# A Fourier mixing layer and a SoLU feed-forward on one core: every second unit's down product as seven block products

## The chip, the cores and the metric

The kernel runs on one core of a Trainium2 chip. The metric is the device time of one execution in microseconds (us); the time before is the median of three runs. Five engines work side by side, each in the order of its own instructions, and wait for each other by semaphores: TensorE (PE in the profile; its weight loads are listed apart as PEld), VectorE (DVE), ScalarE (ACT), GpSimd (POOL) and SyncE (SP), which here only issues transfers.

## The reference

```python
# x: (8, 3136, 256) float32
X = np.fft.fft(np.fft.fft(x, axis=1), axis=2).real     # mixing
x = X.reshape(25088, 256)
h = x @ w_in                                           # 256 -> 1024, "up"
e = np.exp(h - max(h)); sm = e / (sum(e) + 1e-9)       # over the 1024 of a row
solu = h * sm
ln = (solu - mean(solu)) / sqrt(var(solu) + 1e-6) * g_ln
out = ln @ w_out                                       # 1024 -> 256, "down"
```

Everything is float32.

## The kernel before

The sequence of 3136 is 49 x 64. A first transform (over 49) is written to DRAM and read back turned (`turn`); a second one (over 64) gives tiles `q` of 128 tokens. The transform over the 256 features is folded into `w_in`. Two of the eight sequences make a pair; there are four pairs of 25 *units*. A unit stands for one frequency `k1` and its mirror: both share the even and the odd part of `h`, so a unit has two *signs* (the unit with `k1 = 0` has one), and each sign is 128 tokens x 1024.

```python
units = [Unit(p, k1) for p in range(NP) for k1 in range(NK)]     # 4 x 25 = 100
lag = 4

def up(t, c):                       # c = 0: even part, c = 1: odd part; 512 columns a matmul
    for half in range(2):
        nc.tensor.matmul(ps[:, fs], t.q[:, c * P : (c + 1) * P], Wi[:, c, fs], ...)

def spread(t):                      # one value of q to all partitions, by SyncE's queue
    nc.sync.dma_start(out=t.r, in_=t.q[0:1, P : 2 * P])

def even(t, ps):                    # VectorE: ev = w_mid * r + (even part)
    nc.vector.scalar_tensor_tensor(out=t.ev, in0=w_mid, scalar=t.r, in1=ps, ...)

def join(t, ps):                    # VectorE: both signs of h, and the row maxima
def expo(t):                        # ScalarE: u = exp(h - max), both signs, with the sums
def product(t, s):                  # VectorE: u = h * u, with the sums
def square(t, s):                   # ScalarE: sums of squares
def stats(t):                       # GpSimd: five small instructions, then rs = v ** -0.5

def turn_blocks(t, s):              # VectorE: 32 x 32 transposes of u into v
    nc.vector.transpose(out=t.batch.v[:, t.w, :, o], in_=t.u[s])

def move_blocks(batch, units, engines=(nc.sync,)):     # 16 transfers finish the transposition
    for i in range(4):
        for q in range(4):
            engines[i % len(engines)].dma_start(out=uT[b, i], in_=v[a, q])

def down(t, s):                     # 8 matmuls of 256 columns
    ps = ps_m.tile([P, D], FP32, tag="m", name="ps_o")
    for c in range(KF):
        nc.tensor.matmul(ps, uT[:, c, :, s], Wo[:, c, :], start=(c == 0), stop=(c == KF - 1))

def scale(t, s, ps):                # ScalarE: ot = rs * ps
```

Two units share a batch, that is one buffer `v` and one buffer `uT`; of each there are two. PSUM holds the even and the odd part (two banks each) and four more banks, `ps_m`, which all other products take in turn. The steps run over the units; a step works on unit `i` and on the down products of unit `i - 4`:

```python
for i in range(len(units) + lag):
    store(units[i - lag - 1])                    # output rows of an older unit
    even(cur, up(cur, 0)); cur.odd = up(cur, 1)  # begin(i)
    take2(nxt, transform2(...)); spread(nxt)     # q and r of unit i + 2
    join(cur, cur.odd)
    expo(cur)
    ahead_pe(...)                                # a first transform of the next pair, in some steps
    ps_o = [down(old, s) for s in order]
    for s in cur.signs: product(cur, s)
    for s in cur.signs: square(cur, s); turn_blocks(cur, s)
    scale(old, order[0], ps_o[0])
    if cur.w: move_blocks(batches[-1], slice(0, 2))   # after the second unit of a batch
    stats(cur)
    ahead(...)                                   # loads and folds for the next pair
    scale(old, order[1], ps_o[1])
# (cut: the first four units, the last two, the setup of weights and tables)
```

Of the kernel before, what the change touches and what calls it, by code (L numbers as in the profile page):

```python
# [17 lines left out]
P = 128  # L18
# [17 lines left out]
def kernel(  # L36
# [34 lines left out]
    gpool = ctx.enter_context(tc.tile_pool(name="gpool", bufs=6))  # L71
# [5 lines left out]
    ps_m = ctx.enter_context(tc.tile_pool(name="ps_m", bufs=4, space=PSUM))  # L77
# [5 lines left out]
    Wo = const.tile([P, KF, D], FP32, name="Wo")  # L83
    ones = const.tile([P, P], FP32, name="ones")
# [7 lines left out]

    class Pair:
        def __init__(self, p):
            self.p = p
            self.raw, self.y, self.y0 = {}, {}, None
            self.g, self.zs = {}, {}
# [45 lines left out]
    def transform1(pr, s):  # L145

        c, l = divmod(2 * s, CH)
        if s == 0:  # L150
            pr.zd = dram.tile([ZR, NH, D], FP32, tag="zd", name="zd")
        if l == 0:

            if pr.p or c < 2:
                pr.z = zpool.tile([ZR, CH, D], FP32, tag="z", name="z")
            elif c < 4:
                z = fpool.tile([P, FF], FP32, tag="u", name="z_u", bufs=2)
                pr.z = z[0:ZR].rearrange("p (l d) -> p l d", l=CH)
            else:
                pr.z = gpool.tile([P, KG, D], FP32, tag="g", name="z_g")[0:ZR, 0:CH, :]  # L160
            pr.zs[c] = pr.z
        y = pr.y[c]
        ps = ps_m.tile([P, 2, D], FP32, tag="m", name="ps1")
        if s == NH // 2 - 1:
            parts = [(ps[0:ZR, 0], y[:, l], 0), (ps[0:ZR, 1], pr.y0[:, 0], 1), (ps[0:ZR, 1], y[:, l + 1], 2)]
        else:
            parts = [(ps[0:ZR], y[:, l : l + 2], 0)]
        first = True
        for o, i, t in parts:
            for h, cs in enumerate((EVEN, ODD)):  # L170
                nc.tensor.matmul(o[..., cs], F[:, 2 * t + h, :], i[..., cs], start=first, stop=True,  # L171
                                 skip_group_check=True)
                first = False
        nc.scalar.copy(pr.z[:, l : l + 2, :], ps[0:ZR])
        if l == CH - 2:
            keep(pr, c, slice(0, ZR if pr.p else 4 * KG))
# [12 lines left out]
    def transform2(pr, k1):  # L189

        i, k = divmod(k1, KG)
        g = pr.g[i]
        table = T[0][:, :, k, :] if i == 0 else T[1][:, :, k1 - KG, :]
        ps = ps_m.tile([P, KD * P], FP32, tag="m", name="ps2")
        for h in range(KD):
            o = ps[:, h * P : (h + 1) * P].rearrange("p (b k) -> p b k", b=2)
            nc.tensor.matmul(o, g[:, k, h * P : (h + 1) * P], table,  # L199
                             start=(h == 0), stop=True, skip_group_check=True)  # L200
        return ps
# [34 lines left out]
    def join(t, ps):  # L236

        t.nmax = small.tile([P, 2], FP32, tag="nmax", name="nmax")
        for s in t.signs:
            t.h[s] = fpool.tile([P, FF], FP32, tag="h", name="h", bufs=2)  # L240
            nc.vector.tensor_tensor_reduce(out=t.h[s], in0=t.h[0] if s else t.ev, in1=ps,  # L241
                                           scale=1.0 if s else -0.5, scalar=-3.0e38, op0=ALU.add, op1=ALU.max,
                                           accum_out=t.nmax[:, s : s + 1])

    def expo(t):
        t.esum = small.tile([P, 2], FP32, tag="esum", name="esum")
        t.neg = small.tile([P, 2], FP32, tag="neg", name="neg")
        for s in t.signs:
            nc.scalar.mul(out=t.neg[:, s : s + 1], in_=t.nmax[:, s : s + 1], mul=-1.0)  # L249
            t.u[s] = fpool.tile([P, FF], FP32, tag="u", name="u", bufs=2)  # L250
            nc.scalar.activation(out=t.u[s], in_=t.h[s], func=ACT.Exp, bias=t.neg[:, s : s + 1],  # L251
                                 accum_out=t.esum[:, s : s + 1])
# [15 lines left out]
    def stats(t):  # L268

        n = slice(0, len(t.signs))  # L270
        es = small.tile([P, 2], FP32, tag="es", name="es")
        nc.gpsimd.tensor_scalar(out=es[:, n], in0=t.esum[:, n], scalar1=1e-9, scalar2=1e-3,  # L272
                                op0=ALU.add, op1=ALU.mult)
        es2 = small.tile([P, 2], FP32, tag="es2", name="es2")
        nc.gpsimd.tensor_tensor(out=es2[:, n], in0=es[:, n], in1=es[:, n], op=ALU.mult)
        v = small.tile([P, 2], FP32, tag="v", name="v")
        nc.gpsimd.tensor_scalar(out=v[:, n], in0=t.ssq[:, n], scalar1=float(FF) ** -3, scalar2=None, op0=ALU.mult)  # L277
        nc.gpsimd.tensor_tensor(out=v[:, n], in0=v[:, n], in1=es2[:, n], op=ALU.add)
        t.rs = small.tile([P, 2], FP32, tag="rs", name="rs")
        nc.gpsimd.tensor_tensor(out=t.rs[:, n], in0=v[:, n], in1=neg_half[:, n], op=ALU.pow)  # L280
# [14 lines left out]
    def turn_whole(t):  # L295
# [4 lines left out]
        for s in t.signs:  # L300
            for half in range(2):
                ps = ps_m.tile([P, n, P], FP32, tag="m", name="ps_t")
# [17 lines left out]

    def down(t, s):
        uT = t.batch.uT[:, t.w].rearrange("p c i (n s) -> p c (i n) s", s=2)
        ps = ps_m.tile([P, D], FP32, tag="m", name="ps_o")
        for c in range(KF):
            nc.tensor.matmul(ps, uT[:, c, :, s], Wo[:, c, :], start=(c == 0), stop=(c == KF - 1))  # L325
        return ps

    def scale(t, s, ps):
        t.ot[s] = fpool.tile([P, D], FP32, tag="ot", name="ot", bufs=6)
        nc.scalar.mul(out=t.ot[s], in_=ps, mul=t.rs[:, s : s + 1])  # L330
# [21 lines left out]
    mantissa = const.tile([P, NW], I32, name="mantissa")  # L352
    limits = const.tile([P, 3], FP32, name="limits")
# [12 lines left out]
    def exponent(w, raw):  # L366

        if w.dtype == FP32:
            return None
        unit = qpool.tile([P, NW], I32, tag="unit", name="unit", bufs=3)  # L370
        bits(unit, raw[:, 1 : 2 * NW : 2], 20, ALU.logical_shift_right, 0x7FF, ALU.bitwise_and)
        return unit
# [36 lines left out]
    class Weights:  # L409
# [72 lines left out]
        def centre(self):  # L482

            cs = ps_m.tile([P, D], FP32, tag="m", name="cs")
# [25 lines left out]
    def ahead_pe(pr, step):  # L510
# [5 lines left out]
        if 0 <= step - 20 < NK // KG:  # L516
            turn(pr, step - 20)

    with tc.manual_schedule():
# [24 lines left out]
        for i, limit in enumerate((-896.0, 255.0, 255.0 * 2.0 ** 23)):  # L544
# [57 lines left out]
        def begin(i):  # L602

            cur = units[i]
            if i % 2 == 0:
                batches.append(Batch(i >= whole))
            cur.batch, cur.w = batches[-1], i % 2
            even(cur, up(cur, 0))
            cur.odd = up(cur, 1)
            if i + 2 < len(units):  # L610
                nxt = units[i + 2]
                take2(nxt, transform2(pairs[nxt.p], nxt.k1))
                spread(nxt)
# [3 lines left out]
        for i in range(len(units) + lag):  # L617
            cur = units[i] if i < len(units) else None
            old = units[i - lag] if i >= lag else None
            ahd = pairs[cur.p + 1] if cur and cur.p + 1 < NP else None  # L620
            last = i >= len(units) - 2
            prv = units[i - 1] if 0 < i <= whole else None
            if i > lag:
                store(units[i - lag - 1])
            if cur and i > whole:
                begin(i)
            if prv:
                turn_whole(prv)
            if cur:
                join(cur, cur.odd)  # L630
# [3 lines left out]
            if cur:  # L634
                expo(cur)
            if ahd:
                ahead_pe(ahd, cur.k1)
            if old:
                order = old.signs[::-1] if old is units[-1] else old.signs
                ps_o = [down(old, s) for s in order]  # L640
            if i == 0:

                weights.narrow_out(3)
            if cur:
                for s in cur.signs:
                    product(cur, s)
                    if i < whole and s == 0:
                        square(cur, s)
                if i == 1:
                    weights.centre()  # L650
                if i < whole:

                    begin(i + 1)
                for s in cur.signs:
                    if i >= whole or s:
                        square(cur, s)
                    if i >= whole:
                        turn_blocks(cur, s)
            if old:
                scale(old, order[0], ps_o[0])  # L660
            if cur:
                if last:
                    move_blocks(batches[-1], slice(cur.w, cur.w + 1), (nc.sync, nc.gpsimd) if cur.w else (nc.sync,))
                elif cur.w and i >= whole:
                    move_blocks(batches[-1], slice(0, 2))
                stats(cur)
            if i == 0:
                turn(first, 1, nc.sync)
            elif i in (5, 8, 11):
                turn(first, (i + 1) // 3)  # L670
            if ahd:
                ahead(ahd, cur.k1)
            if old and 1 in old.signs:
                scale(old, order[1], ps_o[1])
        store(units[-1])
# [76 lines left out]
```

## Time and profile before

| | before |
|---|---|
| median of three runs | 1188.7 us (1187.45 to 1188.8) |
| span in the profile | 1189.0 us |
| granted TensorE clock | 1.00 |
| uT moves | 752 transfers of 128 KB and 32 of 64 KB |
| SyncE's queue (q1) | 444608 packets, 146.22 MB |
| GpSimd's queue (q0) | 13760 packets, 38.16 MB |

How to read the lines below. In the first part of the page each engine has its busy time, the share of the span and the number of instructions. The chain that ended last is followed back from the last instruction to what released each step, and gives shares of the span by engine and by source line. A line of the timeline has the start, the time from the first start to the last end, the engine (SPq is SyncE's queue), the source line of the kernel, the operation, output <- inputs, the shape and the number merged. In brackets stands the idle time before it and who ended it. The ends of matmuls are modelled and overlap the next one's start, so the pace is read from start to start.

Source lines before: L227 `up`, L199 second transform, L171 first transform, L325 `down`, L233 `even`, L241 `join`, L258 `product`, L293 transposes, L319 `move_blocks`, L210 `spread`, L341 and L337 stores, L330 `scale`.

### The profile page before, as it was taken

Reading aid. Unit: us, or ns where it says so; the run is one execution under the profiler, and the core shown is the slowest. Engines: PE = TensorE matmul, PEld = TensorE weight load, DVE = VectorE, ACT = ScalarE, POOL = GpSimd, SP = SyncE. Lnnn points to the kernel's source line nnn. Section 1 sums busy time; section 2 is a strip of 40 time slices with the busy share of each in tenths; the row PEclk is TensorE's granted clock in tenths of the full one; section 3 lists DMA queues with packets and bytes.
Section 4 is the critical chain, followed back from the end, with each engine's and each line's share of the span. In section 5 each row is a group of like instructions: output and inputs, shape, how many; then the busy total and the mean of one; then the engine's idle time right before and its main releaser. Section 6 shows DMA issues by size and latency. Waiting matters only on the chain.

```text
span 1189.0 us, 15738 instructions
## 1 busy us (share of the span) xinstructions
PE 1152.6 (97%) x4720; PEld 874.5 (74%) x4720; DVE 912.3 (77%) x1234; ACT 679.9 (57%) x1404; POOL 505.9 (43%) x766
## 2 busy tenths in 40 slices
PE   2989999999999999999999999999999999999998
PEld 1556777778777777777777777777777777777787
DVE  6879777777768877787778978777786887877780
ACT  3566665656546656565556656565564665655561
POOL 3025556444544444442644554443553333333323
PEclk9999999999999999999999999999999999999999
DMA  9671989958996766655996887775897464554544
GB/s 231 199 188 27 191 187 193 196 138 165 176 168 165 178 168 167 164 137 140 175 176 170 176 170 166 160 165 133 152 187 142 108 154 97 137 122 116 135 104 117
DMA packets 458452, 185.37 MB, mean 156 GB/s; under 512 B 425750, under 2 KB 440350, under 8 KB 458368
## 3 DMA queue, kind: packets, MB, share of 16 engines
q1 hardware_dynamic: 444608, 146.22, 58.3%
q0 software_dynamic: 13760, 38.16, 12.9%
q8 instruction: 38, 0.62, 0.2%
q14 instruction: 46, 0.38, 0.1%
HBM read 44.78 MB, written 38.80 MB: 70 GB/s over the span
## 4 chain that ended last, share of the span: by engine, by line
PE 93%; DMA 3%; DVE 2%; SPq 1%; issue 1%; POOL 1%; ACT 0%; DVEq 0%; ACTq 0%; POOLq 0%
PE ps_o L325 56%; PE ps_h L227 28%; PE ps L171 5%; PE ps L199 4%; DMA raw_in<-in_moe_w_in_dram 2%; PE wps L456 1%; DMA r<-q 1%; SPq L179 1%; DVE h L241 0%; POOL uT L319 0%; DMA out_dram<-ot,idx 0%; DVE y L123 0%; SPq L442 0%; PE ps_t L305 0%; DVE xa L131 0%
## 5 line engine op out<-in xcount | busy, mean ns | idle before, releaser
L325 PE MATMUL ps_o<-Wo,uT 128*128 128x256 f32 x3136 | 693.4, 379 | 1.3 <-ACT uT L310 0.9
L325 PEld LDWEIGHTS ps_o<-Wo,uT 128*128 128x128 f32 x3136 | 610.8, 196 | 64.0 <-ACT uT L310 1.1
L227 PE MATMUL ps_h<-Wi,q 128*128 128x512 f32 x800 | 360.5, 593 | 5.1 <-DVE ev L233 3.0
L272 POOL TENSOR_SCALAR es<-esum 128x2 f32<-128x2 f32 (+1 forms) x100 | 116.4, 1164 | 425.3 <-ACT u L251 425.1
L258 DVE SCALAR_TENSOR_TENSOR u<-h,u 128x1024 f32<-128x1024 f32 x196 | 239.9, 1225 | 33.5 <-ACT u L251 20.7
L227 PEld LDWEIGHTS ps_h<-Wi,q 128*128 128x128 f32 x800 | 151.5, 190 | 154.3 <-issue 142.3
L265 ACT ACTIVATE h<-u,usum 128x1024 f32<-128x1024 f32 x196 | 224.5, 1147 | 14.8 <-DVE u L258 9.0
L233 DVE SCALAR_TENSOR_TENSOR ev<-w_mid,r,ps_h 128x1024 f32<-128x1024 f32 x100 | 127.8, 1278 | 135.0 <-PE ps_h L227 127.1
L251 ACT ACTIVATE u<-h,neg 128x1024 f32<-128x1024 f32 x196 | 225.6, 1151 | 6.4
L293 DVE STREAM_TRANSPOSE v<-u 128x1024 f32<-128x1024 f32 x192 | 227.5, 1224 | 0.1
L205 ACT COPY q<-ps 128x256 f32<-128x256 f32 x100 | 37.1, 372 | 306.7 <-PE ps L199 279.5
L241 DVE CUSTOM_DVE_ANT_0 h<-ev,ps_h 128x1024 f32<-128x1024 f32 x100 | 122.1, 1221 | 48.9 <-PE ps_h L227 45.3
L330 ACT ACTIVATE ot<-ps_o,rs 128x256 f32<-128x256 f32 x196 | 90.6, 465 | 75.3 <-PE ps_o L325 66.3
L241 DVE CUSTOM_DVE_ANT_0 h<-h,ps_h 128x1024 f32<-128x1024 f32 x96 | 117.3, 1222 | 14.2 <-ACT neg L249 0.5
L337 POOL DMA_INDIRECT out_dram<-ot,idx x96 | 103.1, 1074 | 41.9 <-issue 21.4
L171 PE MATMUL ps<-y,F 98*100 98x258 f32 (+3 forms) x288 | 72.5, 389 | 25.2 <-DVE y L124 25.2
L199 PEld LDWEIGHTS ps<-T,g 128*128 128x128 f32 x400 | 60.2, 191 | 47.4 <-issue 46.9
L249 ACT ACTIVATE neg<-nmax 128x1 f32<-128x1 f32 x196 | 38.8, 198 | 71.0 <-DVE nmax L241 70.9
L280 POOL TENSOR_TENSOR rs<-v,neg_half 128x2 f32<-128x2 f32 (+1 forms) x100 | 71.7, 717 | 7.8
L171 PEld LDWEIGHTS ps<-y,F 98*100 98x100 f32 x288 | 46.3, 179 | 37.6 <-DVE y L124 24.3
L277 POOL TENSOR_SCALAR v<-ssq 128x2 f32<-128x2 f32 (+1 forms) x100 | 22.9, 229 | 117.7 <-ACT h L265 117.6
L199 PE MATMUL ps<-T,g 128*128 128x128 f32 x400 | 60.6, 274 | 0.0
(72 smaller groups left out, 493.9 us busy)
## 6 DMA issues: line engine op xcount, KB each, us to landing
uT<-v SPq DMA_DIRECT2D x752, 128.0 KB
out_dram<-ot SPq DMA_DIRECT2D x100, 128.0 KB
g<-zd POOLq DMA_DIRECT2D x72, 160.0 KB, 5.5
xa<-in_x_dram SPq DMA_DIRECT2D x28, 392.0 KB
zd<-z SPq DMA_DIRECT2D x24, 400.0 KB
raw_in<-in_moe_w_in_dram SPq DMA_DIRECT2D x4, 512.0 KB
raw_out<-in_moe_w_out_dram SPq DMA_DIRECT2D x2, 1024.0 KB
r<-q SPq DMA_DIRECT2D x100, 0.5 KB
```

Of the source, the lines that this page charges most:

```text
L171: nc.tensor.matmul(o[..., cs], F[:, 2 * t + h, :], i[..., cs], start=first, stop=True, skip_group_check=True)
L199: nc.tensor.matmul(o, g[:, k, h * P : (h + 1) * P], table, start=(h == 0), stop=True, skip_group_check=True)
L227: nc.tensor.matmul(ps[:, fs], t.q[:, c * P : (c + 1) * P], Wi[:, c, fs], start=True, stop=True)
L233: nc.vector.scalar_tensor_tensor(out=t.ev, in0=w_mid, scalar=t.r, in1=ps, op0=ALU.mult, op1=ALU.add)
L241: nc.vector.tensor_tensor_reduce(out=t.h[s], in0=t.h[0] if s else t.ev, in1=ps, scale=1.0 if s else -0.5, scalar=-3.0e38, op0=ALU.add, op1 ...
L251: nc.scalar.activation(out=t.u[s], in_=t.h[s], func=ACT.Exp, bias=t.neg[:, s : s + 1], accum_out=t.esum[:, s : s + 1])
L258: nc.vector.scalar_tensor_tensor(out=t.u[s], in0=t.h[s], scalar=1.0, in1=t.u[s], op0=ALU.mult, op1=ALU.mult, accum_out=t.usum[:, s : s + 1])
L265: nc.scalar.activation(out=t.h[s], in_=t.u[s], func=ACT.Square, bias=t.usum[:, s : s + 1], scale=-float(FF), accum_out=t.ssq[:, s : s + 1])
L272: nc.gpsimd.tensor_scalar(out=es[:, n], in0=t.esum[:, n], scalar1=1e-9, scalar2=1e-3, op0=ALU.add, op1=ALU.mult)
L293: nc.vector.transpose(out=t.batch.v[:, t.w, :, o], in_=t.u[s])
L325: nc.tensor.matmul(ps, uT[:, c, :, s], Wo[:, c, :], start=(c == 0), stop=(c == KF - 1))
L337: dma = nc.gpsimd.indirect_dma_start(out=out, out_offset=bass.IndirectOffsetOnAxis(ap=idx[:, i : i + 1], axis=0), in_=t.ot[s], in_offset=None)
```

## The change

Of every second unit (odd number, two signs, not the last) the two down products are computed together. The two signs are the two block rows of A (each cut into two halves of the 1024), `w_out` is cut 2 x 2 into B, and Winograd's form of Strassen's scheme gives the four blocks of C with seven products in place of eight. A block product is four matmuls of 128 columns. GpSimd makes the sums of A (`sums`) and, once, those of B (`weight_sums`). The products accumulate in three banks kept for good; the transforms and the second sign of the other units share the fourth bank (`result(0)`).

```diff
+    def sums(t):
+        A11, A12, A21, A22 = blocks(t)
+        t.S = spool.tile([P, 3, KF // 2, P], FP32, tag="S", name="S")
+        for o, a, b, op in ((t.S[:, 0], A21, A22, ALU.add), (t.S[:, 1], t.S[:, 0], A11, ALU.subtract),
+                            (A21, A11, A21, ALU.subtract), (t.S[:, 2], A12, t.S[:, 1], ALU.subtract)):
+            nc.gpsimd.tensor_tensor(out=o, in0=a, in1=b, op=op)
+    def product7(o, a, b, start=False):
+        for c in range(KF // 2):
+            nc.tensor.matmul(o, a[:, c], b[:, c], start=start and c == 0, ...)
+    class Down:
+        p1:     product7(C11, A11, Wo[:, 0 : KF // 2, 0:P], True)
+        seed:   nc.scalar.copy(C21, C11)          # the next products add to P1
+        p5:     product7(P53, S[:, 0], Ws[:, 0], True)
+        p6:     product7(C21, S[:, 1], Ws[:, 1])
+        copy5:  nc.scalar.copy(E5, P53)
+        p2:     product7(C11, A12, Wo[:, KF // 2 :, 0:P])
+        copy6:  nc.scalar.copy(X, C21); scale(0, 0, C11)
+        p7:     product7(C21, S3, Ws[:, 2])       # S3 lies in uT, in place of A21
+        sum22:  nc.vector.tensor_tensor(out=C22, in0=C21, in1=E5, op=ALU.add)
+        p3:     product7(P53, S[:, 2], Wo[:, KF // 2 :, P:])
+        sum12:  nc.vector.tensor_tensor(out=C12, in0=P53, in1=X, op=ALU.add)
+        p4:     product7(C21, A22, Ws[:, 3])
+        finish: scale(0, 1, C12); scale(1, 1, C22); scale(1, 0, C21)
```

The steps now come in twos. In an odd step (unit `i - 4` by seven) PE has: both up products and the second transform, P1, the second sign of the even unit before it, P5, P6, a first transform where there is one, P2. In the next, even step: up and second transform, P7, P3, a first transform, the first sign of the even unit `i - 4`, P4. Shortened (`new`: a unit begun, `half`: one to go on with, `plain`: the deferred second sign):

```diff
+            if done: done.finish()
+            if half: half.copy6()
+            if by_seven(i - lag + 1): sums(units[i - lag + 1])
+            even(cur, up(cur, 0)); cur.odd = up(cur, 1)
+            second_transform(i + 2)                 # with spread
+            join(cur, 0)
+            if half: half.p7(); half.sum22()
+            join(cur, 1); expo(cur, 0)
+            if half: half.p3(); half.sum12(); other_pairs(i, ahead_pe)
+            if seven: new.p1(); new.seed()
+            elif old: scaled.append((old, order[0], down(old, order[0]))); late = (old, order[1])
+            expo(cur, 1)
+            if plain: ps_o = down(*plain)
+            if seven: new.p5(); new.p6()
+            if half: half.p4()
+            product(cur, 0); product(cur, 1); square(cur, 0)
+            if plain: scale(*plain, ps_o)
+            square(cur, 1)
+            if seven: new.copy5()
+            if not first_sign: other_pairs(i, ahead_pe)
+            if seven: new.p2()
+            turn_blocks(cur, 0); turn_blocks(cur, 1)
+            if cur.w: move_blocks(batches[-1], slice(0, 2))
+            stats(cur)
+            for t, s, ps_o in scaled: scale(t, s, ps_o)
```

Along with it: most of `stats` goes from GpSimd to ScalarE, the `turn` transfers of the later pairs are spread over steps -5, -3, 2, 6 and 11 of their pair in place of five steps in a row, and some buffers change to make room.

```diff
-    gpool = ctx.enter_context(tc.tile_pool(name="gpool", bufs=6))
+    gpool = ctx.enter_context(tc.tile_pool(name="gpool", bufs=3))
-    ps_m = ctx.enter_context(tc.tile_pool(name="ps_m", bufs=4, space=PSUM))
+    ps_m = ctx.enter_context(tc.tile_pool(name="ps_m", bufs=1, space=PSUM))     # four tags, m0 to m3
-        nc.gpsimd.tensor_scalar(out=es[:, n], in0=t.esum[:, n], scalar1=1e-9, scalar2=1e-3, ...)
-        nc.gpsimd.tensor_tensor(out=es2[:, n], ...)
-        nc.gpsimd.tensor_scalar(out=v[:, n], ...)
-        nc.gpsimd.tensor_tensor(out=v[:, n], ...)
+        nc.scalar.activation(out=es2[:, n], in_=t.esum[:, n], func=ACT.Square, ...)
+        for s in t.signs:
+            nc.scalar.activation(out=v[:, s : s + 1], in_=t.ssq[:, s : s + 1], func=ACT.Identity, ...)
-        if 0 <= step - 20 < NK // KG:
-            turn(pr, step - 20)
+        if step in (-5, -3, 2, 6, 11):
+            turn(pr, (-5, -3, 2, 6, 11).index(step))
```

## The prediction

> **What bounds the kernel now.** I read the page first: the busy shares, then the chain that ended last.
>
> ```profile
> PE 1152.6 (97%) x4720; PEld 874.5 (74%) x4720; DVE 912.3 (77%) x1234; ACT 679.9 (57%) x1404; POOL 505.9 (43%) x766
> ...
> PE 93%; DMA 3%; DVE 2%; SPq 1%; issue 1%; POOL 1%; ACT 0%; DVEq 0%; ACTq 0%; POOLq 0%
> ```
>
> PE is busy 97% of the span and is 93% of the chain; it waits some 36 us in all, most of it in the first 100 us. So the kernel is a row of matmuls, and a matmul saved is time saved as long as nothing new makes PE wait. What one matmul costs is read from PE's timeline in a plain stretch; each fp32 matmul is two records there (3136 for 196 x 8 down products).
>
> ```profile
> 1039.09 3.60 PE L227 MATMUL ps_h<-Wi,q 128*128 128x512 f32 x8
> 1042.53 0.61 PE L199 MATMUL ps<-T,g 128*128 128x128 f32 x4
> 1042.97 7.08 PE L325 MATMUL ps_o<-Wo,uT 128*128 128x256 f32 x32
> 1049.89 0.59 PE L227 MATMUL ps_h<-Wi,q 128*128 128x512 f32 x1
> ```
>
> From start to start: up 3.44 us (8 records, 430 ns each), second transform 0.44 (4, 110 ns), down 6.92 (32, 216 ns). A step is 10.80 us, a "double step" of an odd and an even one 21.6. About every second step also has a first transform: four records of 258 and 254 columns, 0.85 us.
>
> Next I read who feeds the stages: SyncE's timeline, then VectorE's and ScalarE's in the same stretch.
>
> ```profile
> 1028.96 13.20 SPq L319 DMA_DIRECT2D uT<-v  x16
> 1042.26 1.21 SPq L341 DMA_DIRECT2D out_dram<-ot  x1
> 1043.57 0.63 SPq L210 DMA_DIRECT2D r<-q  x1
> ...
> 1050.55 4.11 SPq L319 DMA_DIRECT2D uT<-v  x5
> ```
>
> ```profile
> 1041.01 1.28 DVE L233 SCALAR_TENSOR_TENSOR ev<-w_mid,r,ps_h 128x1024 f32<-128x1024 f32 x1 [1.32 <-PE ps_h L227]
> ...
> 1048.12 2.37 DVE L293 STREAM_TRANSPOSE v<-u 128x1024 f32<-128x1024 f32 x2
> 1051.80 1.28 DVE L233 SCALAR_TENSOR_TENSOR ev<-w_mid,r,ps_h 128x1024 f32<-128x1024 f32 x1 [1.32 <-PE ps_h L227]
> ```
>
> Once a double step SyncE issues the 16 block moves of uT; they take it 13.2 us. The little transfer r, which `even` needs, stands behind them and a store: issued 14.6 us after the first move, read by ev at 1051.80. Of those 8.2 us it needs about 2 (below): r has some 6 us to spare. The moves begin when the transposes of the second unit end (1028.9), early in the step after it.
>
> **What the Trainium skill says.** "TensorE: Matmul & The Clock Gate", section LDWEIGHTS: a weight load takes its columns divided by 1.2, in ns, 107 for 128 columns, about what a 128-column fp32 record streams for. The records of the second transform agree: loads 190 ns long, but started every 110 ns and overlapping. "DMA: Bandwidth & Descriptors", section Anatomy of one DMA: about 2 us of a small DMA is fixed cost, mostly the write receipt. Agreed: at its quickest, for the first unit, ev starts 2.2 us after r's issue (58.9 to 61.0); where the transfers are crowded 3.6 (133.1 to 136.8). "SBUF — State Buffer", section Who interferes with whom: a VectorE operation with two SBUF inputs contends with a GpSimd one that reads SBUF. The trace shows no cost: the product of h and u takes 1212 to 1230 ns in all 196 cases.
>
> **The change, part by part.** *Block products.* By seven go the odd units 1 to 97 that have two signs, 47 of them. Down before: 32 records of 216 = 6.91 us. After: 7 products x 4 chunks x 2 records x 111 = 6.22. Saved 0.70 us of PE a double step, 47 x 0.70 = 33 us. The even step becomes up 3.44, transform 0.44, P7 0.89, P3 0.89, sign 0 down 3.46, P4 0.89: 10.0 us. The odd step: up and transform 3.88, P1 0.89, the deferred sign 1 down 3.46, P5, P6, P2 2.66: 10.9 us. A double step is 20.9.
>
> *Other engines.* ScalarE: seed and two copies (0.3 each, from 373 ns for 256 columns), four scalings of 128 columns for two of 256 (about 0.35 for 0.465), statistics three instructions of 0.2 a step: about +115 us, 680 to 795, two thirds of the span. VectorE: two adds of about 0.3 a double step, +28 us. GpSimd: four sums of 128x512 a double step, about 1.2 us each (2341 ns for 1020 columns), +220, less some 180 of statistics. None is full; what counts is the order.
>
> *What moves.* uT has two buffers. Before, the moves into one waited for the downs of the odd unit, which ended as the odd step did. Now P7, P3 and P4 of that unit lie in the next even step, and P7 and P4 read uT. In the built program the first move waits for P4's last matmul. So the moves begin one whole step later, and SyncE, in order, holds r behind them.
>
> Let S be the start of the odd step after P4. Moves from S+0.3. r issued at S+0.3+14.4 = S+14.7, landed 2.2 to 2.5 later: S+17.1. The even step begins at S+10.9; its ev would start 1.9 into it (1041.01 against 1039.09), at S+12.8. **It now waits 4.3 us for r.**
>
> From ev on, with E its start, back to back: join 1 at E+1.3, add, join 2 at E+3.0, add, products at E+4.6 and E+6.0 (starts are 1.37 apart before too), square of the second ends E+8.5, statistics E+9.1, sign 0 scaling E+9.6 (frees P1's bank), the three finishing scalings E+10.5, the copy of q E+11.0. The deferred down uses the transform's bank, so it waits for that copy. PE by itself would reach it 14.8 us after the even step's start (10.0 + 3.88 + 0.89). With E 6.2 after that start it comes 6.2 + 11.0 - 14.8 = 2.4 us too late. A wait there puts off the next even step, which shortens the next one, so two waits in a row share 2.4 us: 1.2 on average. Double step: 20.9 + 1.2 = **22.1 against 21.6**. Over 47 double steps about +24 us.
>
> *The loaded stretches.* The same chain with a slower burst:
>
> ```profile
> 298.58 16.00 SPq L319 DMA_DIRECT2D uT<-v  x16
> 314.68 1.33 SPq L341 DMA_DIRECT2D out_dram<-ot  x1
> 316.11 0.66 SPq L210 DMA_DIRECT2D r<-q  x1
> ```
>
> Here a `turn` of g runs beside the moves (DMA share 1.12 in 300 to 320 us, 0.72 in 1052 to 1066) and r goes out 17.5 us after the first move; in the first five bursts 17 to 20 us, with 3.6 us to land. Before, that was hidden. Now uT's own landing counts as well: sign 0 down stands at S+16.5 (S+18.2 with two first transforms); a quiet burst's packets end 16.1 us after its first issue, those of loaded ones 19 to 22. The change spreads the turns, one to a burst in 15 bursts, so I take 1 us more for each (half of the 2 us or so that a turn lengthens a burst, as the next wait gives some back), and 3 us for each of the first five double steps: 30. Of this I count less than half, 13, since transfers spread over longer double steps collide less; that factor is a guess. Sum: 1188.7 + 24 + 13 = **1225 us**.
>
> **The rivals.** *PE stays the bound*: 1188.7 - 33 = 1156. For it: 97% busy, all other engines under 80%, and a change that places its products with care. Against it: the place of P4 and the order on SyncE. It would need r or the ScalarE chain some 2.5 us a double step earlier than I count. *Weight loads bind*: at 190 ns each, 56 of them take 10.6 us, 3.7 more a unit, 1363 us. Against it: records 110 apart in the transform. A smaller share is open, as half the stationary tiles are read at a step of two elements (loads 196 against 190 ns): at most 0.2 us a double step, 10 us. *The moves themselves bind, not r*: then the wait is at sign 0 down, nothing in quiet double steps and about 1.5 us in some 20 loaded ones: 1156 + 30, about 1185.
>
> **Range and chances.** A quiet double step may be 21.3 (chain 1.5 us shorter) to 22.9: -14 to +61 us over 47; with loaded ones -8 to +73. I give 1180 to 1262. Faster by 2% needs a double step of about 21.0, nearly no wait: 0.10. Within 2%: 0.33. Slower: 0.57.
>
> **What would show it.** Right: block records 110 to 112 ns apart; uT's first move just after P4; `ev <- DMA r` of some 150 to 250 us in VectorE's waits (7.7 before); PE idle before the deferred down or P1, released by ScalarE's q or ot; PE's busy time down 33 us but its share near 91 to 94%; double steps of 22 us late in the run and over 24 early on. Wrong: PE at 97% and double steps of 21.0, or PE waiting on DMA uT alone, or block records 130 ns and more apart.

## The result, and the profile after

The changed kernel takes 1302.1 us (median of four runs, 1298.3 to 1306.3) against 1188.8 us before. The ratio is 1.0955, with a 95% interval of 1.0911 to 1.0999: it is slower by 113 us, where the prediction had 37.

The first part of the page, and from the second the clock granted in 40 slices of the span (1296.4 us):

```profile
PE 1172.7 (90%) x5850; PEld 899.5 (69%) x5850; DVE 948.3 (73%) x1329; ACT 775.4 (60%) x1935; POOL 587.7 (45%) x558
...
PEclk9999999999998999999999999899999999999998
```

PE has less arithmetic to do than before, and is busy 20 us *longer* (1172.7 against 1152.6). One cause is the clock: it falls below full speed in several slices (mean 0.984), and a matmul at half clock counts as busy for twice as long (the 16 records of P5 and P6 from 1270.5 us took 3.6 us in place of 1.8). Some 35 us of PE's busy time lie in such stretches, so the clock accounts for about 17 us. Another 10 us are weights read at a step of two elements (below); the rest was not taken apart. Idle time has grown as well, from 36 to 124 us.

VectorE's largest wait, and then PE's own waits (engine, line <- who ended it: total us, times, longest):

```profile
DVE ev L244 <- DMA r<-q: 197.6, 40, 9.8
```

```profile
PE ps_m L355 <- ACT ot L436: 27.6, 25, 2.3
...
PE ps_m L182 <- ACT ot L436: 16.6, 17, 1.7
PE ps_m L355 <- DVE E L407: 13.3, 6, 5.2
```

L244 is `even`, L355 a block product, L182 the first transform, L431 `down`, L238 `up`, L407 the add `sum22`, L436 and L424 the scalings of `down` and of the blocks, L326 the moves, L221 `spread`, L447 a store, L216 the copy of q, L115 a load, L198 a `turn`. `even` waits for r 4.9 us on average, in 40 of its 100 cases. PE meets the delay in three places: at P1, whose bank ScalarE frees late; at the odd step's first transform, where the bank still holds the deferred second sign until ScalarE has scaled it; and at P4, whose bank waits for `sum22`, which stands behind `ev` on VectorE.

A quiet double step late in the run, on PE, SyncE, VectorE and ScalarE in turn:

```profile
1132.90 1.21 PE L355 MATMUL ps_m<-Wo,uT 128*128 128x128 f32 x8 [1.19 <-ACT ot L436]
...
1144.16 1.11 PE L355 MATMUL ps_m<-Ws,uT 128*128 128x128 f32 x8
1145.11 1.06 PE L355 MATMUL ps_m<-Wo,S 128*128 128x128 f32 x8
1146.00 3.62 PE L431 MATMUL ps_m<-Wo,uT 128*128 128x256 f32 x16
1149.46 1.10 PE L355 MATMUL ps_m<-Ws,uT 128*128 128x128 f32 x8
1150.40 3.60 PE L238 MATMUL ps_h<-Wi,q 128*128 128x512 f32 x8
```

```profile
1127.91 13.46 SPq L326 DMA_DIRECT2D uT<-v  x16
1141.41 0.79 SPq L447 DMA_DIRECT2D out_dram<-ot  x1
1142.30 0.90 SPq L221 DMA_DIRECT2D r<-q  x1
...
1150.64 8.23 SPq L326 DMA_DIRECT2D uT<-v  x10
```

```profile
1144.99 1.28 DVE L244 SCALAR_TENSOR_TENSOR ev<-w_mid,r,ps_h 128x1024 f32<-128x1024 f32 x1 [2.99 <-DMA r<-q]
```

```profile
1153.91 0.45 ACT L436 ACTIVATE ot<-ps_m,rs 128x256 f32<-128x256 f32 x1
...
1155.10 0.36 ACT L216 COPY q<-ps_m 128x256 f32<-128x256 f32 x1
```

The moves start 0.24 us after the odd step's up products, which follow P4 (1150.40, 1150.64). r goes out 14.4 us after the first move, `ev` reads it 2.7 us later and has waited 3.0 us. The scaling that frees P1's bank starts 8.9 us after `ev`, the copy of q 10.1 us after. From start to start, P7 and P4, whose weights lie in `uT`, take 0.95 and 0.94 us, and P3, whose weights lie in S, 0.89 us.

The double step with the longest wait for r, one that has loads: SyncE, a `turn` by GpSimd, then `ev`, then P4, then the three stretches around (columns: window and its length, busy time and number of instructions of PE, PEld, DVE, ACT and POOL, then clock, DMA share, GB/s):

```profile
371.73 13.89 SPq L326 DMA_DIRECT2D uT<-v  x16
385.66 1.35 SPq L115 DMA_DIRECT2D xa<-in_x_dram  x2
387.06 0.38 SPq L447 DMA_DIRECT2D out_dram<-ot  x1
387.53 0.53 SPq L221 DMA_DIRECT2D r<-q  x1
```

```profile
386.51 2.42 POOL L198 DMA_DIRECT2D g<-zd  x4
```

```profile
395.66 1.28 DVE L244 SCALAR_TENSOR_TENSOR ev<-w_mid,r,ps_h 128x1024 f32<-128x1024 f32 x1 [9.84 <-DMA r<-q]
```

```profile
398.61 2.07 PE L355 MATMUL ps_m<-Ws,uT 128*128 128x128 f32 x8 [5.17 <-DVE E L407]
400.47 5.42 PE L238 MATMUL ps_h<-Wi,q 128*128 128x512 f32 x8
```

```profile
390.50:397.30 6.80, 2.94 (x14) 2.33 (x12) 1.46 (x2) 0.00 (x0) 3.59 (x3) 1.00 0.69 157
397.30:404.10 6.80, 5.50 (x13) 3.43 (x14) 6.66 (x12) 5.49 (x12) 0.00 (x0) 0.50 0.20 44
404.10:411.00 6.90, 6.90 (x31) 5.51 (x31) 6.41 (x9) 4.40 (x13) 3.12 (x3) 1.00 0.77 173
```

The burst of moves is no longer than a quiet one (13.9 us). But two loads of 392 KB come between it and r, GpSimd issues the four transfers of a `turn` (160 KB each) at the same time, and from r's issue to `ev` it takes 8.1 us: at the 157 GB/s of the first stretch the two loads alone are 5 us. PE stands for 5.2 us before P4, and then the clock is at 0.50 for 6.8 us, in which the eight up matmul records take 5.3 us instead of 3.4. So one late r costs PE twice, once in waiting and once in speed.

The length of every double step is the distance between the starts of the odd steps' up products on PE's timeline (47 of them), against 21.6 us quiet and 23.3 loaded before. The extra time is: the last nine, without loads, +8.7 us; twelve without first transforms, eight of them with a `turn`, +26; 23 with first transforms and most with loads, +48; three with the one-sign unit, +10; what follows the start of the last of them, +16 (there PE stands 6.3 us for GpSimd's sums of the last unit by seven, and the clock is halved for 6.8); the start, -1.5. Together 107 us, which is the whole difference of the two spans (1296.4 and 1189.0).

### The profile page after: what moved, and what is told of

It reads as the page before. It is cut to its first block, busy times and chain, and to the rows that moved or that the text cites. A ratio compares the mean times of both kernels' runs of the same rounds, so it can differ in the third digit from the quotient of the medians.

```text
span 1296.4 us, 18631 instructions
## 1 busy us (share of the span) xinstructions
PE 1172.7 (90%) x5850; PEld 899.5 (69%) x5850; DVE 948.3 (73%) x1329; ACT 775.4 (60%) x1935; POOL 587.7 (45%) x558
## 5 line engine op out<-in xcount | busy, mean ns | idle before, releaser
L431 PE MATMUL ps_m<-Wo,uT 128*128 128x256 f32 x1632 | 378.0, 385 | 15.3 <-DMA r<-q 4.7
L238 PE MATMUL ps_h<-Wi,q 128*128 128x512 f32 x800 | 366.4, 601 | 2.5 <-DVE nmax L252 1.6
L431 PEld LDWEIGHTS ps_m<-Wo,uT 128*128 128x128 f32 x1632 | 316.9, 198 | 52.0 <-issue 12.8
L268 DVE SCALAR_TENSOR_TENSOR u<-h,u 128x1024 f32<-128x1024 f32 x196 | 262.7, 1347 | 39.4 <-ACT u L261 37.5
L244 DVE SCALAR_TENSOR_TENSOR ev<-w_mid,r,ps_h 128x1024 f32<-128x1024 f32 x100 | 126.6, 1266 | 225.1 <-DMA r<-q 197.6
L238 PEld LDWEIGHTS ps_h<-Wi,q 128*128 128x128 f32 x800 | 147.3, 194 | 150.9 <-issue 141.6
L252 DVE CUSTOM_DVE_ANT_0 h<-ev,ps_h 128x1024 f32<-128x1024 f32 x100 | 122.2, 1222 | 19.8 <-DVE ev L244 9.3
L355 PE MATMUL ps_m<-Wo,uT 128*128 128x128 f32 x752 | 109.5, 290 | 27.7 <-ACT ot L436 27.6
L355 PEld LDWEIGHTS ps_m<-Wo,uT 128*128 128x128 f32 x752 | 99.9, 200 | 35.4 <-ACT ot L436 33.6
L355 PE MATMUL ps_m<-Ws,uT 128*128 128x128 f32 x752 | 107.4, 287 | 15.4 <-DVE E L407 13.3
L216 ACT COPY q<-ps_m 128x256 f32<-128x256 f32 x100 | 36.6, 366 | 137.7 <-PE ps_m L210 137.7
L355 PEld LDWEIGHTS ps_m<-Ws,uT 128*128 128x128 f32 x752 | 100.7, 200 | 21.9 <-DVE E L407 18.0
L182 PE MATMUL ps_m<-y,F 98*100 98x258 f32 (+3 forms) x288 | 74.6, 395 | 43.2 <-DVE y L130 24.3
L355 PE MATMUL ps_m<-Ws,S 128*128 128x128 f32 x752 | 94.1, 278 | 10.7 <-POOL S L350 6.3
L355 PEld LDWEIGHTS ps_m<-Ws,S 128*128 128x128 f32 x752 | 93.0, 195 | 13.3 <-POOL S L350 6.5
```

Source lines behind the costliest of these rows:

```text
L268: nc.vector.scalar_tensor_tensor(out=t.u[s], in0=t.h[s], scalar=1.0, in1=t.u[s], op0=ALU.mult, op1=ALU.mult, accum_out=t.usum[:, s : s + 1])
L355: nc.tensor.matmul(o, a[:, c], b[:, c], start=start and c == 0, stop=c == n - 1, skip_group_check=True)
```

## The experiments

| | what it changes | us | ratio to before, 95% interval |
|---|---|---|---|
| e1_order | r and stores ahead of the moves | 1246.9 | 1.0466 (1.0432 to 1.0500) |
| e2_r_act | r by ScalarE's queue | 1582.5 | 1.3303 (1.3280 to 1.3325) |
| e3_free_ut | P7 and P4 don't read uT | 1186.2 | 0.9971 (0.9960 to 0.9982) |
| e4_no_seven | no blocks, sign still deferred | 1337.2 | 1.1226 (1.1186 to 1.1265) |
| e5_slots | uT free early, whole computation | 1194.1 | 1.0041 (1.0021 to 1.0061) |
| e6_t1_tail | e5, first transform behind P2, plain end | 1183.8 | 0.9960 (0.9950 to 0.9970) |
| e7_no_defer | no blocks, nothing deferred | 1237.4 | 1.0406 (1.0384 to 1.0427) |
| e8_no_sums | GpSimd's sums left out | 1295.5 | 1.0873 (1.0842 to 1.0904) |
| e9_t1 | only the first transform behind P2 | 1286.7 | 1.0821 (1.0783 to 1.0858) |

**e1_order: r ahead of the moves.** The moves are recorded one step later, behind P4. They could not start earlier anyway; only the order on SyncE changes.

```diff
+            if pend: move_blocks(pend, slice(0, 2)); pend = None      # behind p4, before the transposes
-                 elif cur.w: move_blocks(batches[-1], slice(0, 2))
+                 elif cur.w: pend = batches[-1]
```

> The 16 moves of a batch are recorded one step later, after P4 of the even step, so that SyncE issues the two r and the stores ahead of them; the moves themselves can start no earlier than before, since P4 holds them. Theory A (r behind the moves is what delays VectorE, ScalarE and then PE): VectorE's wait for r falls from 198 us to under 20, a quiet double step from 22.1 to 21.0 to 21.4, PE's waits at P1 and at the first transform of the odd step shrink to a few us, the clock stays at 1.00, time 1190 to 1225. Theory B (uT's own landing binds): nothing is gained, the wait only moves to the first-sign down of the even step, time over 1270. Theory C (strided weight loads, the shared bank and ScalarE's extra work are the cost): over 1250.

```profile
1117.67 1.15 SPq L221 DMA_DIRECT2D r<-q  x1
...
1125.11 13.11 SPq L326 DMA_DIRECT2D uT<-v  x16
```

1246.9 us, 55 less than the changed kernel, but above the range of theory A, and the clock is at 0.986 instead of 1.00. The wait of `ev` for r is gone from VectorE's waits; PE's gaps before P1 fall from some 31 to 1 us (from step 5 on, each counted from start to start); quiet double steps take 21.1. What stays is a new wait, of nearly 40 us, before the even step's first-sign `down`. The page names various releasers for it, but it ends 3 to 8 us after the last move's issue, on semaphores that moves use: those are the moves themselves, whose data land late. So r behind the moves is about half of the loss, and the moves' late start most of the other half.

**e2_r_act: r by another queue.**

```diff
-        nc.sync.dma_start(out=t.r, in_=t.q[0:1, P : 2 * P])
+        nc.scalar.dma_start(out=t.r, in_=t.q[0:1, P : 2 * P])
```

> r is issued by ScalarE right after its copy of q; all else as in the changed kernel. A: as in the run with the order changed, perhaps 10 to 40 us more, as ScalarE spends about 0.5 us of each step on the issue: 1195 to 1260. B: about 1300, no change. C: about 1300 or more, as ScalarE has still more to do.

1582.5 us, and both expectations fall. A quiet stretch on SyncE and its issues on ScalarE's queue, then PE, shows why:

```profile
1407.86 10.10 SPq L326 DMA_DIRECT2D uT<-v  x12
...
1425.08 2.63 SPq L326 DMA_DIRECT2D uT<-v  x4
```

```profile
1423.12 0.48 ACTq L221 DMA_DIRECT2D r<-q  x1
```

```profile
1431.18 6.52 PE L431 MATMUL ps_m<-Wo,uT 128*128 128x256 f32 x16 [6.67 <-DMA out_dram<-ot]
```

Twelve moves go out, then SyncE stands for 7.1 us, and the last four follow 2.0 us after ScalarE has issued an r. In the trace SyncE's and ScalarE's transfers use eight completion semaphores in turn, and the thirteenth move waits on the one that this r signals (number 102): r is issued by ScalarE only when its step's q has been copied, and until it has landed the burst stands. It takes 19.8 us from first issue to last in place of 13.5, and such pauses of 2 to 9 us come 52 times in the run. PE names a store as its releaser, but it is the last four moves that it waited for, at half clock afterwards (16 records in 6.4 us). So this run says nothing against r as the cause, nor for it: it took one wait away and made a longer one in the moves.

**e3_free_ut: uT free at the end of the odd step.** P7 and P4 read S in place of `uT`. Their products are of other blocks, so the rows of the units by seven aren't the reference's; the number and size of all instructions stay.

```diff
-            product7(self.C21, self.S3, Ws[:, 2])
+            product7(self.C21, self.t.S[:, 0], Ws[:, 2])
-            product7(self.C21, self.A22, Ws[:, 3])
+            product7(self.C21, self.t.S[:, 1], Ws[:, 3])
```

> P7 and P4 read two of the S tiles in place of the two blocks in uT (so the output is not the reference's); nothing in the even step reads the odd unit's uT any more, and the moves can start at the end of the odd step as they did in the kernel before. Also P7 and P4 load weights without a step. A and B alike: r and uT come early, VectorE's wait for r under 20 us, a quiet double step 20.9 to 21.2, time 1165 to 1195. Below the run with the order changed by more than 15 us would say that uT's landing (B) is a part of the cost besides r. C: over 1240.

```profile
PE 1131.8 (96%) x5850; PEld 879.8 (74%) x5850; DVE 973.7 (82%) x1329; ACT 784.5 (66%) x1935; POOL 621.1 (53%) x558
```

1186.2 us, as expected. With the two reads away the whole loss of 113 us is gone and 3 us more (some 5 of these 116 because P7 and P4 now read their weights without a step), the clock is at 0.999, quiet double steps take 21.0 and loaded ones 22.7 to 22.8. The spread turns are still there, and so are ScalarE's extra work and GpSimd's sums. None of them costs much where r and `uT` come early; what they cost beside a late r was not tried alone (a run with the turns at their old steps is missing).

**e4_no_seven and e7_no_defer: the deferral without the blocks, and neither.** In e4 no unit goes by seven, but the second sign of every unit is still deferred by one step; in e7 it is not deferred. In e4 the sum made in place for the first unit stays, so that unit's rows aren't the reference's.

```diff
         def by_seven(i):
-            return i % 2 and i < len(units) - 1 and len(units[i].signs) == 2
+            return False
```

```diff
-            if i == whole: sums(units[1])                    # e7 alone
-                late = (old, order[1]) if len(order) == 2 else None
+                if len(order) == 2: plain = (old, order[1])
```

> No unit goes by seven; everything else of the change stays (deferred second sign, one bank for transforms and second signs, statistics on ScalarE, turns spread out, fewer buffers). PE has 33 us more of matmul time than the changed kernel. A: nothing holds the moves beyond the odd step or, with the deferred sign of the odd unit, the down in the next step, so r is partly late: 1190 to 1225. Theory D (the surroundings of the block products cost the time): 1270 or more. C: in between, about 1240.

> No unit by seven and no second sign deferred; the banks, the statistics on ScalarE, the spread turns and the smaller buffers of the change stay. The moves start at the end of the odd step as before. A: 1188 to 1210, near the kernel before, whereas with the deferral it was 1337. Theory D (these surroundings cost the time by themselves): over 1250.

e4 takes 1337.2 us, more than the changed kernel, and I had expected less than 1225; e7 takes 1237.4, for which 1188 to 1210 was expected.

```profile
DVE ev L244 <- DMA r<-q: 224.8, 39, 9.9
```

```profile
PE ps_m L182 <- ACT ot L436: 24.8, 44, 0.6
```

The first line is from e4: r is as late there without a single block product, since the odd unit's deferred second sign reads `uT` in the next step just as P4 did. I had taken the blocks for what holds the buffer; it is any product of the odd unit that reads it in the even step. Between e4 and e7, which differ in the deferral, lie 100 us. The second line is from e7: no wait for r, quiet double steps of 21.6 us exactly as before, and loaded ones of 24.9 (23.3 before), because each of 44 first transforms now follows a second sign in the same single bank and waits for its scaling (some 0.7 us each from start to start). So the statistics on ScalarE, the pools and the order of the steps cost nothing where they don't meet that bank.

**e5_slots: the same with the whole computation.** S3 and a copy of A22 (GpSimd) get room of their own, from two buffers of `ot` and one of `q`; the two sums of P5 and P6 now have one buffer.

```diff
+        t.Sa = spool.tile([P, 2, KF // 2, P], FP32, tag="Sa", name="Sa", bufs=1)   # sums for P5, P6
         ... (A21 in place of itself becomes t.S[:, 0]; S[:, 0], S[:, 1] become Sa[:, 0], Sa[:, 1])
+        nc.gpsimd.tensor_copy(out=t.S[:, 1], in_=A22)
-            product7(self.C21, self.S3, Ws[:, 2])         # p7
+            product7(self.C21, self.t.S[:, 0], Ws[:, 2])
-            product7(self.C21, self.A22, Ws[:, 3])        # p4
+            product7(self.C21, self.t.S[:, 1], Ws[:, 3])
```

> The whole computation, with one more tile: A11-A21 goes into a tile of its own and A22 is copied beside it by GpSimd, so that P7 and P4 no longer read uT (room: the first two sums in one buffer, two ot and one q buffer less). As in the run that let P7 and P4 read S, the moves can start at the end of the odd step: VectorE's wait for r under 20 us, a quiet double step of 21.0 to 21.2, time 1180 to 1195. If GpSimd's extra copy (some 0.7 to 1.5 us a double step) or its contention with VectorE mattered, 1200 or more.

1194.1 us. The loss is gone but for 5 us, at the price of one more GpSimd instruction a double step. This is e3's reading without e3's exchanged blocks.

**e6_t1_tail: e5, and the two smaller waits.** The odd step's first transform goes behind P2, and unit 97, the last by seven, goes plainly.

```diff
-            if cur and not first_sign: other_pairs(i, ahead_pe)
             if seven: new.p2(); half = new
+            if cur and not first_sign: other_pairs(i, ahead_pe)
-            return i % 2 and i < len(units) - 1 and len(units[i].signs) == 2
+            return i % 2 and i < len(units) - 3 and len(units[i].signs) == 2
```

> As the run before this one, with the odd step's first transform behind P2 (so that the bank it shares with the deferred second sign has 0.9 us more to come free), and unit 97 in the plain way. PE's wait at that transform (6 us in five steps where moves are early) goes, and some 3 to 5 us at the end: 4 to 12 us less than the run before this one, 1170 to 1188. If the single bank costs nothing once r is early: no difference beyond the end's.

1183.8 us: the interval of the ratio lies below 1, and this is the fastest run of the whole computation, though by 0.4% only. Its page, a double step on PE, and SyncE:

```profile
PE 1135.0 (96%) x5826; PEld 880.8 (75%) x5826; DVE 987.4 (84%) x1327; ACT 784.6 (66%) x1930; POOL 674.1 (57%) x600
```

```profile
1048.60 3.60 PE L238 MATMUL ps_h<-Wi,q 128*128 128x512 f32 x8
...
1059.61 3.60 PE L238 MATMUL ps_h<-Wi,q 128*128 128x512 f32 x8
```

```profile
1039.38 13.10 SPq L326 DMA_DIRECT2D uT<-v  x16
1052.52 0.78 SPq L449 DMA_DIRECT2D out_dram<-ot  x1
1053.40 0.69 SPq L221 DMA_DIRECT2D r<-q  x1
```

The moves start with the even step again (1039.38), and r is issued 8 us before `ev` of the next even step reads it at 1061.53. An odd step takes 11.01 us without a wait. PE is busy 17.6 us less than before the change.

**e8_no_sums: GpSimd's sums left out.** They are made for the first unit by seven alone and its S is used by all others, so the rows of those aren't the reference's; PE does the same work.

```diff
+        if kept: t.S = kept[0]; return
```

> The changed kernel, but GpSimd makes the sums for the first unit by seven only; later units use that unit's S (left out: their sums; the output is not the reference's). If GpSimd's reads beside VectorE's products of h and u (mean 1347 ns, 1225 before) are a main cost: below 1260. A and B: the products go back to about 1226 ns, and the time falls by 0 to 20 us, 1280 to 1302, since the moves start as late as ever.

1295.5 us, 7 us less, and the two sets of runs overlap (1288.7 to 1300.5 against 1298.3 to 1306.3). VectorE's product of h and u (count, then busy us and mean ns) in the changed kernel and in e8:

```profile
L268 DVE SCALAR_TENSOR_TENSOR u<-h,u 128x1024 f32<-128x1024 f32 x196 | 262.7, 1347 | 39.4 <-ACT u L261 37.5
```

```profile
L268 DVE SCALAR_TENSOR_TENSOR u<-h,u 128x1024 f32<-128x1024 f32 x196 | 244.2, 1248 | 47.5 <-ACT u L261 43.2 <-issue 0.7
```

It was 1225 ns before, is 1347 beside the sums, and 1248 without them. The contention is real and small.

**e9_t1: the first transform alone.** The first part of e6's diff, on the changed kernel.

> Only the odd step's first transform goes behind P2, so that PE no longer stands at the single bank in front of it; the moves and r stay late. In the changed kernel that wait took 18.6 us in 16 places. Theory (r behind the late moves is the main cause, and a wait taken away ahead of it only moves to the next place where the VectorE and ScalarE chain is late): the time falls by less than the wait, 5 to 15 us, to about 1287 to 1297; ev's wait for r stays at 190 to 215 us; PE's wait at P1 grows above 30. Rival (the single bank is a cause of its own, and drives the clock's halving too): the time falls by 20 us or more, to 1282 or less, with the clock mean up from 0.984 to 0.99.

1286.7 us, 15 us less, for a wait that took 18.6 us from start to start. Both expectations are half right: the wait is worth nearly its own size, so the single bank is a cause of its own, but the clock's mean stays at 0.984, `ev` still waits 176.5 us for r, and P1's gap is hardly larger (some 32 us).

Not tried: a third `uT` buffer of 16 KB a partition, which should let all moves start as before.

## Why the prediction was wrong, by its own steps

- *PE is the bound, and the block products save 0.70 us a double step.* Held nearly: S-fed block products run at 111 ns a record. Those with weights from `uT` need 118, the step of two elements that the prediction left open; the four of them cost 0.2 us a double step, the whole 10 us it had named as the most. A double step without a wait is 21.0 us (e3, e5, e6) for the predicted 20.9.
- *The moves wait for P4, and r behind them.* Right in each link: first move at S+0.24 (S+0.3), r issued at S+14.6 (S+14.7), `ev` waiting 3.0 to 5.7 us (4.3) in the quiet stretch.
- *From `ev` to the copy of q 11.0 us.* Measured 10.1; the scaling at 8.9 for 9.6. PE's first wait is at P1, not at the deferred `down`. The prediction's own numbers say so: PE by itself reaches P1 13.9 us after the even step's start (10.0 + 3.88), and the bank comes free at 6.2 + 9.6 = 15.8.
- *Quiet double step 22.1.* The number is right, in part by luck: from 1150.6 to 1194.8, first move to first move, two of them take 22.1 each; the last eight average 22.2, and one more, 25.4, has a `turn` and a stretch at half clock in it. But the waits in those two are 0.14 and 1.26 us at P1, 0.7 on average where 1.2 was predicted; the weights' step adds 0.2, and P1 and the deferred sign run 0.27 us slower than P2 and the first sign (1.10 and 3.57 us for 0.94 and 3.46), which no step of the prediction has and no run explains.
- *The loaded stretches +13.* **This is the step that failed.** It took a longer burst of moves as the cause, 30 us, and halved it by a guess, "since transfers spread over longer double steps collide less". The sum gave the 38 double steps ahead of the quiet end 38 x 0.5 + 13 = 32 us; they cost 84 (26 + 48 + 10), and what follows the last step's start another 16. The bursts were not the reason: from first issue to last they took 12.6 to 15.4 us in all but one (17.3), less than the 16.0 of the loaded one shown before, and 13 to 14.1 in the first five, for which 3 us more each were allowed. Four things were, none of them in the sum at its size (the first three are waits that overlap and feed one another, so they don't add up to the 84):
  - First, r's own landing: 3.8 us from issue to `ev` on average over the 39 waits that can be paired with an issue, 6.0 to 8.1 in four with a load just ahead, where the prediction used 2.2 to 2.5. A load alone does not explain it: six other r with one just ahead took 3.5 to 4.4, and the two longest (7.0 and 8.1) had a `turn` issued just ahead as well. The trace before already had 3.6, 4.4 and 5.5 us at three of its four waits of `ev` for r. (The 2 us that the prediction quotes is the skill's figure for transfers that GpSimd issues; r is issued by SyncE, so the measured times count.)
  - Second, the odd step's first transform in the shared bank: 18.6 us.
  - Third, P4 behind `sum22` behind `ev`: 14.6 us, because the add stands after `ev` in VectorE's order.
  - Fourth, the clock: about 41 us of the span at half speed, worth about 17 us of matmul time, each time after a wait.
- *VectorE and GpSimd: no cost.* Wrong in principle, small in size. "SBUF — State Buffer", Who interferes with whom, had it right: with sums of two inputs on GpSimd the product's mean went from 1225 to 1347 ns, singly to 2893. In e6 the mean is 1529, and the time does not suffer. The trace before had no such sums beside it, so its silence did not bear on the change.
- *The rivals.* "Moves bind, not r" was worth more than it was given: with r out of the way (e1) the moves' late landing still holds 53 to 61 us (1246.9 against e5's 1194.1 and e3's 1186.2; some 5 of them are the weights' step, which e3 and e5 take out of P7 and P4). "Weight loads bind" is out; a load lasts 190 ns in the trace and not the 107 that the prediction quotes, and what agrees is the pace alone, one load every 110 ns. "PE stays the bound" is what e6 comes nearest to, at 1183.8 for 1156.

The sum from the runs: 1302 us, minus 55 for r's place in the queue, minus 53 to 61 for the time at which `uT` comes free (the moves' landing, and the clock's halving that goes with those waits), gives 1186 to 1194; the first transform's place and the plain end take off 10 more. Of the 33 us that the products save, 10 (5 in e6, where P1 and P2 alone read `uT`) go back to the weights' step. In e6 quiet double steps are 0.6 us shorter than before and loaded ones 0.4; the end is 49.1 us against 42.4. How the rest of the saving divides between the double steps at the change of a pair and the end was not taken apart by a run. Nor was the clock's share separated from the waits that trigger it: no run kept one without the other.

## What to carry to other kernels

When products are postponed, ask which buffer they still read: two reads of `uT` one step later moved 16 transfers by a step, and with them everything behind them in the same queue. Put a small transfer that someone waits for ahead of the bulk in its queue, and move it to another queue only after looking at which completion semaphores the transfers share. A wait of PE of 2 us and more can cost twice (eight of the ten behind step 5 of the changed kernel were followed by half clock), and an estimate of a loaded stretch needs its own landing times, not those of the quiet one.

## What the runs showed of the hardware that was not expected

- The clock can fall after short waits. "TensorE: Matmul & The Clock Gate", Part 1: The HAM clock gate, has half clock after an idle window of about 3.4 us. Here it came after waits of 2.3 us (before 1041.1 us) and 2.7 us (before 769.0 us), and lasted 3.4 or 6.8 us, the same unit. The length of the wait does not decide it: in e4 a wait of 3.3 us (before 352.4 us) was followed by full clock.
- A small transfer can take long where large ones were issued just ahead: r took 2.5 to 3.3 us to `ev` in six of the last eight double steps where `ev` waited, and 8.1 us behind 784 KB of loads, with a `turn` of 640 KB beside them. "DMA: Bandwidth & Descriptors", Queues, rings and completion order, says that a completion's increment lands only after every earlier write of that DMA engine; that agrees with these times, though no run tested it alone.
- Weights read at a step of two elements cost PE 118 ns a record in place of 111.
